# First loads of an S5 + GEGLU kernel: the Gelu table ahead of a weight load on ScalarE, three parameter loads from SyncE to GpSimd

## The chip, the core and the metric

The kernel runs on one core of one Trainium2 chip. A core has TensorE (PE, matmuls), VectorE (DVE), ScalarE (ACT), GpSimd (POOL) and SyncE (SP, which issues DMAs here). ScalarE and GpSimd can issue DMAs too. The metric is device time in microseconds (us); lower is better. The time given for a kernel is the median of its runs.

## The reference, cut to what matters

One batch of L = 2048 rows of D = 512 values is normalized; two branches read the result, and their sum is added to the input.

```python
xn = layernorm(x)                                   # over the 512 values of a row, eps 1e-5
dt = exp(log_dt); Lam_bar = exp(dt * Lam)           # Lam = Lambda_re + 1j * Lambda_im, 512 of them
B_bar = ((Lam_bar - 1) / Lam)[:, None] * Bmat
h[t] = Lam_bar * h[t-1] + B_bar @ xn[t]             # complex recurrence over the 2048 rows
A = 2 * (h @ Cmat.T).real + xn * Dskip
B = (gelu(xn @ w_gate) * (xn @ w_up)) @ w_down      # 512 -> 1376 -> 512
out = x + A + B                                     # bfloat16
```

## The kernel before

**Blocks and stages.** The 2048 rows are four blocks of 512, each of four tiles of 128 rows. For a block b, `LN(b)` computes row statistics (L625, L626), mean and square root (`root`, L628 to L634: a copy and a `pow` on GpSimd, L633 and L632), reciprocal (L637) and the normalized rows XN (`norms`, L644). `TR(b)` transposes these by four DMAs (L722) into XNT[b]. `BU(b)` (L734) multiplies them by B; `CHAIN(b)` turns the recurrence into real scans (L754 to L783, scans at L767) on VectorE. `GU(b)` (L823) makes the gate and up products, and the last 96 of the 1376 columns are made at L797; Gelu and a copy on ScalarE (L838, L841) and a product on VectorE (L843) give the hidden values. `DN(b)` (L863) adds, into PSUM seeded with x, the hidden values times w_down and then the scanned states times C; L881 adds the skip branch and a DMA (L883) stores the tile.

**Block 0 is special.** The start can't wait for DMA transposes. Its tiles are centred (L931, L939; the mean of tile 1 comes from ScalarE, L936), transposed on TensorE (`cent_T`, L673) with the identity tile IDN, and copied by ScalarE (L680). `GT_mm` (L698) then multiplies the centred tiles by the first 896 of 1376 gate and up columns, in "units" of a tile by a column range; `GT_evac` scales by the reciprocal root, applies Gelu (L707) and multiplies (L710). The first gate chunk, columns 0 to 383, comes in two halves of 256 rows of w_gate each (`ld_wg0`, L499). The first four matmuls read half 0, the next four half 1, both for tile 0; eight more multiply tile 1 by gate columns; after these come the up columns (L491). Behind the units TensorE does `GU(0)` for four column tiles, `BU(0)` and `BU(1)`, then `GU(1)` and the rest.

**Set-up.** VectorE sets WRM (L476) and HALF (L478) and makes IDN (L480) from an iota of GpSimd (L479). GpSimd clears the parameter rows PROW (L481) and fills EXB, EPS, HPI, IOTJ and HR (L548 to L552). ScalarE applies Gelu to HALF (L554) early, so that its function table is loaded. TensorE runs seven matmuls on zeros meanwhile (L913).

**Parameters.** `load_par` loads log_dt, Lambda_re and Lambda_im into rows of PROW (L515, 1 KB each); `tr_par` transposes PROW by DMA into PAR (L519). `params` (L567 and on) and `coefs` make the scan's coefficients from it.

**What sets the order.** `Sched` holds all operations with their reads and writes, estimated durations and engine. TensorE's and SyncE's instructions stay in the order in which the code adds them; the others are ordered by a planner, `schedule`, from these durations and from priorities that it works out backward. `emit` writes each engine's program, with a semaphore wait ahead of an operation for each of its producers. A queue is strictly in order: what stands behind a waiting DMA waits with it. `order_behind(op, prev)` keeps an operation behind another of the same engine without a semaphore wait. SyncE's order at the start is: tiles 0 and 1 of x; half 1 of the first gate chunk; tile 2; up chunk 0; tile 3; gate and up chunks 1 and 2; the three parameter loads; gate and up chunks 3; `tr_par`; `TR(0)`; x of block 1 (L485); transposed loads of B_re and B_im (L530); Dskip (L539); x of block 2; `TR(1)`. Half 0 is issued by ScalarE, which waits for IDN first; the Gelu operation has a planner's earliest time of 900 ns (`nb`).

Of the kernel before, what the change touches and what calls it, by code (L numbers as in the profile page):

```python
# [10 lines left out]
ACTF = mybir.ActivationFunctionType  # L11
BF16, F32, I32 = dt.bfloat16, dt.float32, dt.int32
# [347 lines left out]
EPS_BF16 = 1.0013580322265625e-05  # L360
# [6 lines left out]
def d_dve_ts4x(n): return 220.0 + 0.26 * n  # L367
# [5 lines left out]
def build(nc, ins, out):  # L373
    with ExitStack() as es:
        E = es.enter_context
        S = Sched(nc, es)
        ARENA_BYTES = 207 * 1024
        arena_t = E(nc.sbuf_tensor("arena", [128, ARENA_BYTES // 2], BF16))
        A = Arena(arena_t, ARENA_BYTES)
# [6 lines left out]
        WG = A.alloc("WG", [KD, F], BF16)  # L386
# [30 lines left out]
        HALF = A.alloc("HALF", [4], F32)  # L417
# [11 lines left out]
        PROWq = [Buf("PROW%d" % q, "prow", q, q + 1) for q in range(3)]  # L429
# [3 lines left out]
        EXB = A.alloc("EXB", [KP], F32)  # L433
        HPI = A.alloc("HPI", [1], F32)
        EPS = A.alloc("EPS", [1], F32)
# [15 lines left out]
        HR = A.alloc("HR", [4, 128], BF16)  # L451
        HRp = [A.sub(A.alloc("HRv", [2, 256], BF16, at=HR.lo), "HR%d" % i, i) for i in range(2)]
# [8 lines left out]
        IOTJ = A.alloc("IOTJ", [512], I32, at=OUTB_all.lo)  # L461
# [8 lines left out]

        V = lambda fn, dur, r, w, tag="", after=(): S.op("vector", fn, dur, r, w, tag, after)
        ACT = lambda fn, dur, r, w, tag="", after=(): S.op("scalar", fn, dur, r, w, tag, after)
        POOL = lambda fn, dur, r, w, tag="": S.op("gpsimd", fn, dur, r, w, tag)
        PE = lambda fn, dur, r, w, tag="": S.op("tensor", fn, dur, r, w, tag)

        V(lambda e: e.memset(WRM.ap, 0.0), 150, [], [WRM], "wrm")  # L476
        GATE = {"before_gelu": [], "nh": 0}
        V(lambda e: e.memset(HALF.ap, 0.5), D_TINY, [], [HALF], "half")  # L478
        POOL(lambda e: e.iota(IOT.ap, [[1, 128]], base=0, channel_multiplier=-1), 300, [], [IOT], "iota")  # L479
        GATE["ident"] = V(lambda e: e.tensor_scalar(IDN.ap, IOT.ap, 0.0, None, ALU.is_equal), d_dve_ts4x(128), [IOT], [IDN], "ident")  # L480
        POOL(lambda e: e.memset(PROW16.ap, 0.0), 100, [], [PROW, *PROWq], "prow0")  # L481
        NM1 = A.alloc("NM1", [1], F32)
# [11 lines left out]
        def ld_x0(j):  # L494
            S.dma(lambda e, j=j: e.dma_start(X[j].ap, x2[128 * j:128 * (j + 1), :]), 128 * 1024, writes=[X[j]], tag="ld_x0")  # L495
        WG0h = [Buf("WG0h%d" % n, "sbx", n / 2, (n + 1) / 2) for n in range(2)]

        def ld_wg0(n, queue, after=()):
            S.dma(lambda e: e.dma_start(WG.ap[:, 2 * n:2 * n + 2, 0:384],  # L499
                                        ins["B_w_gate"][256 * n:256 * (n + 1), 0:384].rearrange("(k p) f -> p k f", p=128)),  # L500
                  192 * 1024, writes=[WG0h[n]], tag="ld_w", queue=queue, after=after)
        ld_x0(0)
        ld_x0(1)
        ld_wg0(0, "scalar", [GATE["ident"]])
        ld_wg0(1, "sync")
        ld_x0(2)
        ld_w(WU, WUc, ins["B_w_up"], 0)
        ld_x0(3)
# [4 lines left out]
        def load_par():  # L513
            for q, nm in enumerate(("A_log_dt", "A_Lambda_re", "A_Lambda_im")):
                S.dma(lambda e, q=q, nm=nm: e.dma_start(PROW.ap[4 * q:4 * q + 4, :], ins[nm].rearrange("(s p) -> s p", p=128)),  # L515
                      1024, writes=[PROWq[q]], tag="ld_" + nm)

        def tr_par():
            S.dma(lambda e: e.dma_start_transpose(PAR.ap.rearrange("p q t -> p (q t)").unsqueeze(1), PROW16.ap), 4096,  # L519
# [25 lines left out]

        wchunk = lambda ft: 0 if ft < 3 else (1 if ft < 5 else (2 if ft < 7 else 3))

        POOL(lambda e: e.memset(EXB.ap, math.e), 100, [], [EXB], "exb")  # L548
        POOL(lambda e: e.memset(EPS.ap, EPS_BF16), 100, [], [EPS], "eps")
        POOL(lambda e: e.memset(HPI.ap, 0.5 * math.pi), 100, [], [HPI], "hpi")  # L550
        POOL(lambda e: e.iota(IOTJ.ap, [[1, 512]], base=0, channel_multiplier=0), 600, [], [IOTJ], "iotj")
        POOL(lambda e: e.memset(HR.ap, 0.0), 300, [], HRp, "hr0")  # L552
        SCR = A.alloc("SCR", [1], F32)
        GATE["table"] = ACT(lambda e: e.activation(SCR.ap, HALF.ap[:, 0:1], ACTF.Gelu_apprx_tanh), 1480, [HALF], [SCR], "gelu0")  # L554
        GATE["table"].nb = 900.0
        rstate = {"n": 0}

        def next_bank():
# [7 lines left out]
        def params():  # L566
            S.order_behind(POOL(lambda e: e.tensor_tensor(DTB.ap, EXB.ap, LDT.ap, ALU.pow), 1100, [EXB, LDT], [DTB], "exp_dt"), GATE["pow"])  # L567
            V(lambda e: e.tensor_tensor(pa(TH), DTB.ap, LIM.ap, ALU.mult), D_TINY, [DTB, LIM], [PA[TH]], "th")
            V(lambda e: e.tensor_tensor(pa(A_), DTB.ap, LRE.ap, ALU.mult), D_TINY, [DTB, LRE], [PA[A_]], "a")
            POOL(lambda e: e.tensor_tensor(pa(RRr), EXB.ap, pa(A_), ALU.pow), 1100, [EXB, PA[A_]], [PA[RRr]], "exp_a")  # L570
            V(lambda e: e.tensor_scalar(w16(0, 4), pa(TH), 1.0 / TWO_PI, None, ALU.mult), D_TINY, [PA[TH]], [W16p[0]])
            V(lambda e: e.tensor_scalar(w16(4, 8), pa(TH), 512.0 / TWO_PI, None, ALU.mult), D_TINY, [PA[TH]], [W16p[1]])
            V(lambda e: e.tensor_scalar(w16(8, 16), w16(0, 8), 0.25, None, ALU.add), D_TINY, W16p[0:2], W16p[2:4])
            V(lambda e: e.tensor_copy(KI.ap, W16.ap), D_TINY, W16p, [KI])
            V(lambda e: e.tensor_tensor(FRC.ap, W16.ap, KI.ap, ALU.subtract), D_TINY, W16p + [KI], [FRC])
# [34 lines left out]
        def tables_dve(behind):  # L610
            for s in range(KP):
                V(lambda e, s=s: e.tensor_scalar(K1s[s].ap, IOTJ.ap, W16.ap[:, s:s + 1], None, ALU.mult),
                  d_dve_ts4x(512) * 1.3, [IOTJ, W16p[0]], [K1s[s]], "k1", [GATE["evTA"]])
                V(lambda e, s=s: e.scalar_tensor_tensor(F1s[s].ap, IOTJ.ap, W16.ap[:, s:s + 1], K1s[s].ap, ALU.mult, ALU.subtract),  # L614
# [315 lines left out]
        def sub(j):  # L930
            return V(lambda e: e.tensor_scalar(XN[j].ap, X[j].ap, MVt[0][j].ap[:, 0:1], None, ALU.subtract),  # L931
                     d_dve_ts4x(512), [X[j], MVt[0][j]], [XN[j]], "sub")
        load_par()
        load_W()
        tr_par()
# [83 lines left out]
def bass_parallel_sum__ssm_conv_s5__geglu_ffn__prompt_kernel(  # L1019
    nc: bass.Bass,  # L1020
    A_x: bass.AP,
    A_Lambda_re: bass.AP,
    A_Lambda_im: bass.AP,
    A_B_re: bass.AP,
    A_B_im: bass.AP,
    A_C_re: bass.AP,
    A_C_im: bass.AP,
    A_log_dt: bass.AP,
    A_Dskip: bass.AP,
    B_x: bass.AP,  # L1030
    B_w_gate: bass.AP,
    B_w_up: bass.AP,
    B_w_down: bass.AP,
    out: bass.AP,
):
    ins = {
        "A_x": A_x, "A_Lambda_re": A_Lambda_re, "A_Lambda_im": A_Lambda_im,
        "A_B_re": A_B_re, "A_B_im": A_B_im, "A_C_re": A_C_re, "A_C_im": A_C_im,
        "A_log_dt": A_log_dt, "A_Dskip": A_Dskip,
        "B_w_gate": B_w_gate, "B_w_up": B_w_up, "B_w_down": B_w_down,  # L1040
    }
    build(nc, ins, out)
# [28 lines left out]
```

## Time and profile before

| | us |
|---|---|
| median of 5 runs | 180.52 |
| lowest, highest | 179.8, 180.85 |
| profiled execution | 180.85 |
| its span in the trace | 179.0 |
| TensorE busy | 173.2 |
| VectorE busy | 160.7 |
| ScalarE busy | 89.4 |
| GpSimd busy | 14.0 |

The profile is of one execution; the span runs from its first to its last recorded instruction. Times in a row are microseconds from the span's start, unless marked ns. In a row of the order of time, the first number is the start, the second the length, then come engine (a q behind it is its queue, which issues DMAs), line, operation and tiles. In a row of waits the numbers are the sum, the count and the longest. L340 is the place where waits are written for all engines. Matmuls overlap in their pipeline, so TensorE's busy time says less than the chain of work that ended last, which is followed back from the end of the kernel. The granted TensorE clock is full in all slices of the page.

### The profile page before, as it was taken

Reading aid. Unit: us, or ns where it says so; the run is one execution under the profiler, and the core shown is the slowest. Engines: PE = TensorE matmul, PEld = TensorE weight load, DVE = VectorE, ACT = ScalarE, POOL = GpSimd, SP = SyncE. Lnnn points to the kernel's source line nnn. Section 1 sums busy time; section 2 is a strip of 40 time slices with the busy share of each in tenths; the row PEclk is TensorE's granted clock in tenths of the full one; section 3 lists DMA queues with packets and bytes.
Section 4 is the critical chain, followed back from the end, with each engine's and each line's share of the span. In section 5 each row is a group of like instructions: output and inputs, shape, how many; then the busy total and the mean of one; then the engine's idle time right before and its main releaser. Section 6 shows DMA issues by size and latency. Waiting matters only on the chain.

```text
span 179.0 us, 2505 instructions
## 1 busy us (share of the span) xinstructions
PE 173.2 (97%) x884; PEld 83.7 (47%) x884; DVE 160.7 (90%) x283; ACT 89.4 (50%) x169; POOL 14.0 (8%) x25
## 2 busy tenths in 40 slices
PE   7799999699999999999999999999999999999994
PEld 3664364244644444444544444444464444444453
DVE  5798898997999979969999999989999999999911
ACT  3475559987776799101676596000567880000000
POOL 3222040209000000200000000000000000000000
PEclk9999999999999999999999999999999999999999
DMA  5994899697599500001105100010001000000321
GB/s 144 290 311 91 187 196 179 91 118 149 109 225 323 126 4 2 0 29 34 54 13 107 29 2 0 24 39 29 29 0 29 4 0 0 0 0 10 112 78 41
DMA packets 33397, 14.37 MB, mean 80 GB/s; under 512 B 23688, under 2 KB 33384, under 8 KB 33384
## 3 DMA queue, kind: packets, MB, share of 16 engines
q1 hardware_dynamic: 33112, 14.01, 35.0%
q10 hardware_dynamic: 272, 0.20, 0.4%
q8 instruction: 7, 0.11, 0.3%
q14 instruction: 6, 0.05, 0.1%
HBM read 6.46 MB, written 2.10 MB: 48 GB/s over the span
## 4 chain that ended last, share of the span: by engine, by line
PE 84%; DMA 7%; DVE 6%; SPq 1%; issue 1%; ACT 0%; ACTq 0%; DVEq 0%
PE PS L863 37%; PE PS L823 29%; PE PS L734 12%; PE PS L698 4%; DMA arena<-in_B_w_up_dram 3%; DMA arena<-in_A_x_dram 2%; PE PS L797 2%; DMA arena<-arena 2%; DVE arena L625 1%; DVE arena L710 1%; DVE arena L644 1%; DVE arena L614 1%; SPq L495 1%; DVE arena L616 1%; DVE arena L843 0%
## 5 line engine op out<-in xcount | busy, mean ns | idle before, releaser
L863 PE MATMUL PS<-arena 128*128 128x512 bf16 (+3 forms) x323 | 66.2, 366 | 0.0
L823 PE MATMUL PS<-arena 128*128 128x512 bf16 x264 | 58.1, 379 | 0.3 <-DMA arena<-arena 0.3
L863 PEld LDWEIGHTS PS<-arena 128*128 128x128 bf16 (+1 forms) x323 | 30.8, 98 | 35.3
L823 PEld LDWEIGHTS PS<-arena 128*128 128x128 bf16 x264 | 25.7, 98 | 30.9 <-issue 0.7
L767 DVE TENSOR_TENSOR_SCAN arena<-arena 128x512 bf16<-128x512 f32 x32 | 38.7, 1251 | 0.0
L838 ACT ACTIVATE arena<-PS 128x512 bf16<-128x512 f32 x33 | 19.8, 601 | 37.4 <-PE PS L823 33.8
L734 PE MATMUL PS<-arena 128*128 128x512 bf16 x128 | 28.3, 379 | 1.4 <-DMA arena<-arena 1.4
L841 ACT ACTIVATE arena<-PS 128x512 bf16<-128x512 f32 x33 | 19.7, 598 | 5.2 <-PE PS L823 4.9
L734 PEld LDWEIGHTS PS<-arena 128*128 128x128 bf16 x128 | 12.5, 98 | 16.5 <-issue 1.9
L738 ACT ACTIVATE arena<-PS 128x512 bf16<-128x512 f32 x32 | 17.6, 596 | 1.3 <-PE PS L734 1.3
L855 ACT ACTIVATE PS<-arena 128x512 f32<-128x512 bf16 (+2 forms) x17 | 9.3, 580 | 17.8 <-DVE arena L881 17.1
L881 DVE TENSOR_TENSOR arena<-PS,arena 128x512 bf16<-128x512 f32 (+2 forms) x17 | 10.8, 651 | 8.2 <-PE PS L863 8.1
L843 DVE TENSOR_TENSOR arena<-arena 128x512 bf16<-128x512 bf16 x33 | 13.0, 411 | 1.5 <-ACT arena L841 1.5
L698 PE MATMUL PS<-arena 128*128 128x192 bf16 (+2 forms) x80 | 12.8, 315 | 0.4 <-DMA arena<-in_B_w_gate_dram 0.3
L625 DVE BATCH_NORM_STATS2 arena<-arena 128x6 f32<-128x512 bf16 x16 | 10.3, 682 | 2.9 <-DMA arena<-in_A_x_dram 2.9
L698 PEld LDWEIGHTS PS<-arena 128*128 128x128 bf16 x80 | 7.1, 98 | 5.3 <-DMA arena<-in_B_w_gate_dram 0.5
L754 DVE TENSOR_TENSOR arena<-arena 128x4096 bf16<-128x4096 bf16 (+1 forms) x5 | 9.2, 1854 | 0.0
L756 DVE TENSOR_TENSOR arena<-arena 128x4096 bf16<-128x4096 bf16 (+1 forms) x5 | 9.2, 1852 | 0.0
L780 DVE TENSOR_TENSOR arena<-arena 128x4096 bf16<-128x4096 bf16 x4 | 9.1, 2284 | 0.0
L779 DVE TENSOR_TENSOR arena<-arena 128x4096 bf16<-128x4096 bf16 x4 | 9.1, 2283 | 0.0
L707 ACT ACTIVATE arena<-PS,arena 128x192 bf16<-128x192 f32 (+1 forms) x16 | 6.7, 449 | 3.0 <-PE PS L698 2.6
L710 DVE SCALAR_TENSOR_TENSOR arena<-PS,arena 128x192 bf16<-128x192 f32 (+1 forms) x16 | 6.9, 448 | 0.7 <-ACT arena L707 0.4
(84 smaller groups left out, 113.7 us busy)
## 6 DMA issues: line engine op xcount, KB each, us to landing
out_dram<-arena SPq DMA_DIRECT2D x15, 128.0 KB, 1.7
arena<-in_A_x_dram SPq DMA_DIRECT2D x3, 512.0 KB, 5.5
arena<-in_B_w_down_dram SPq DMA_DIRECT2D x1, 1280.0 KB, 7.2
arena<-in_A_x_dram SPq DMA_DIRECT2D x4, 128.0 KB, 2.8
arena<-in_B_w_gate_dram SPq DMA_DIRECT2D x2, 256.0 KB, 5.5
arena<-in_B_w_up_dram SPq DMA_DIRECT2D x2, 256.0 KB, 5.8
arena<-in_B_w_gate_dram SPq DMA_DIRECT2D x1, 480.0 KB, 4.3
arena<-in_B_w_up_dram SPq DMA_DIRECT2D x1, 480.0 KB, 5.2
```

Of the source, the lines that this page charges most:

```text
L625: return (V(lambda e: e.bn_stats(ST[tt].ap, X[tt].ap), d_dve_1x(512), [X[tt]], [ST[tt]], "bnst"), V(lambda e: e.bn_aggr(MVt[b][j].ap, ST[t ...
L698: ins_ = e.matmul(dst, XCd(j, k), WGU[:, us[0]:us[-1] + 1, k, f0:f1], start=(k == 0), stop=(k == KD - 1))
L734: ins_ = e.matmul(PS[bank][:, :], BBT[c][dk].ap[:, 128 * s:128 * (s + 1)], XNT[b].ap[:, dk, :], start=(dk == 0), stop=(dk == KD - 1))
L738: ACT(lambda e, bank=bank, k3=k3, s=s, c=c: e.activation(SSc[k3][s][c].ap, PS[bank][:, :], ACTF.Copy), d_act(512), [BANK[bank]], [SSc[k3][ ...
L767: V(lambda e, g=g, rb=rb, init=init: e.tensor_tensor_scan(g.ap, rb, g.ap, init, ALU.mult, ALU.add), d_dve_scan(512), [g, PA[RRr]] + ([CARc ...
L823: ins_ = e.matmul(PS[bank][0:m, c0:c1], W.ap[:, dk, 128 * ft:128 * ft + m], XNT[b].ap[:, dk, c0:c1], start=(dk == 0), stop=(dk == KD - 1))
L838: GATE["last_gelu"] = ACT(lambda e, bg=bg, kk=kk, m=m: e.activation(GG[kk].ap[0:m, :], PS[bg][0:m, :], ACTF.Gelu_apprx_tanh), d_act(512), ...
L841: ACT(lambda e, bu=bu, kk=kk, m=m: e.activation(UPB[kk].ap[0:m, :], PS[bu][0:m, :], ACTF.Copy), d_act(512), [BANK[bu]], [UPB[kk]], "evU")
L843: V(lambda e, kk=kk, m=m, ft=ft, k2=k2: e.tensor_tensor(HTt[k2][ft].ap[0:m, :], GG[kk].ap[0:m, :], UPB[kk].ap[0:m, :], ALU.mult), d_dve_tt ...
L855: ACT(lambda e: e.activation(PS[bank][:, c0:c1], X[tt].ap[:, c0:c1], ACTF.Copy), d_act(c1 - c0), [X[tt]], [BANK[bank]], "seed")
L863: ins_ = e.matmul(PS[bank][:, c0:c1], l_[:, 128 * j:128 * (j + 1)], r_[:, c0:c1], start=False, stop=last and n == len(ops) - 1, skip_group ...
L881: V(lambda e: e.tensor_tensor(OUTB[ko].ap[:, c0:c1], PS[bank][:, c0:c1], XD[tt].ap[:, c0:c1], ALU.add), d_dve_1x(c1 - c0), [BANK[bank], XD ...
```

## The change

The Gelu operation that loads ScalarE's table moves to the start of the program and becomes ready with HALF; its earliest time of 900 ns goes. Half 0 of the first gate chunk is issued by SyncE, in half 1's old place; half 1 is issued by ScalarE, in order behind the Gelu operation, without waiting for IDN. The three parameter loads are issued by GpSimd. GpSimd's EXB, EPS, HPI, IOTJ and HR wait for IDN. What is computed is the same.

```diff
-        POOL = lambda fn, dur, r, w, tag="": S.op("gpsimd", fn, dur, r, w, tag)
+        POOL = lambda fn, dur, r, w, tag="", after=(): S.op("gpsimd", fn, dur, r, w, tag, after)
...
+        SCR = A.alloc("SCR", [1], F32)
         V(lambda e: e.memset(HALF.ap, 0.5), D_TINY, [], [HALF], "half")
+        GATE["table"] = ACT(lambda e: e.activation(SCR.ap, HALF.ap[:, 0:1], ACTF.Gelu_apprx_tanh), 1480, [HALF], [SCR], "gelu0")
...
         def ld_wg0(n, queue, after=()):
-            S.dma(lambda e: e.dma_start(WG.ap[:, 2 * n:2 * n + 2, 0:384],
+            return S.dma(lambda e: e.dma_start(WG.ap[:, 2 * n:2 * n + 2, 0:384],
...
-        ld_wg0(0, "scalar", [GATE["ident"]])
-        ld_wg0(1, "sync")
+        ld_wg0(0, "sync")
+        S.order_behind(ld_wg0(1, "scalar"), GATE["table"])
...
-                      1024, writes=[PROWq[q]], tag="ld_" + nm)
+                      1024, writes=[PROWq[q]], tag="ld_" + nm, queue="gpsimd")
...
-        POOL(lambda e: e.memset(EXB.ap, math.e), 100, [], [EXB], "exb")
-        POOL(lambda e: e.memset(EPS.ap, EPS_BF16), 100, [], [EPS], "eps")
-        POOL(lambda e: e.memset(HPI.ap, 0.5 * math.pi), 100, [], [HPI], "hpi")
-        POOL(lambda e: e.iota(IOTJ.ap, [[1, 512]], base=0, channel_multiplier=0), 600, [], [IOTJ], "iotj")
-        POOL(lambda e: e.memset(HR.ap, 0.0), 300, [], HRp, "hr0")
-        SCR = A.alloc("SCR", [1], F32)
-        GATE["table"] = ACT(lambda e: e.activation(SCR.ap, HALF.ap[:, 0:1], ACTF.Gelu_apprx_tanh), 1480, [HALF], [SCR], "gelu0")
-        GATE["table"].nb = 900.0
+        POOL(lambda e: e.memset(EXB.ap, math.e), 100, [], [EXB], "exb", [GATE["ident"]])
+        POOL(lambda e: e.memset(EPS.ap, EPS_BF16), 100, [], [EPS], "eps", [GATE["ident"]])
+        POOL(lambda e: e.memset(HPI.ap, 0.5 * math.pi), 100, [], [HPI], "hpi", [GATE["ident"]])
+        POOL(lambda e: e.iota(IOTJ.ap, [[1, 512]], base=0, channel_multiplier=0), 600, [], [IOTJ], "iotj", [GATE["ident"]])
+        POOL(lambda e: e.memset(HR.ap, 0.0), 300, [], HRp, "hr0", [GATE["ident"]])
```

## The prediction

> **What bounds the kernel now.** I read the page first, then the chain that ended last, then TensorE's waits, then the order of time of the first 40 us on the queues of SyncE, ScalarE, GpSimd and VectorE.
>
> ```profile
> span 179.0 us, 2505 instructions
> PE 173.2 (97%) x884; PEld 83.7 (47%) x884; DVE 160.7 (90%) x283; ACT 89.4 (50%) x169; POOL 14.0 (8%) x25
> ...
> PE 84%; DMA 7%; DVE 6%; SPq 1%; issue 1%; ACT 0%; ACTq 0%; DVEq 0%
> ```
>
> A busy share of 97% is not yet a bound, since ends of matmuls are modelled. The chain says it better: from 34.39 to 176.77 us it lies on TensorE without a gap, 142.4 us. So the time is the moment at which BU(1) begins (34.39), plus a fixed 142.4, plus the last store. What the change touches lies wholly ahead of that moment. TensorE's waits:
>
> ```profile
> PE PS L734 <- DMA arena<-arena: 1.4, 1, 1.4
> ...
> PE PS L698 <- DMA arena<-in_B_w_gate_dram: 0.3, 1, 0.3
> PE PS L823 <- DMA arena<-arena: 0.3, 1, 0.3
> ```
>
> The chain gives a fourth: 2.63 us issue of the first up chunk (WU chunk 0), landing 5.04 later, at 7.67; TensorE goes on at 7.72. After 7.72 only 0.27 us (GU(0) for the transposes of TR(0)) and 1.39 us (BU(1) for those of TR(1)) are idle. These two are all that can be won behind 7.72, 1.66 us. What holds the transposes is SyncE's queue:
>
> ```profile
> 7.12 0.79 SPq L515 DMA_DIRECT2D arena<-in_A_log_dt_dram  x1
> ...
> 7.96 0.26 SPq L515 DMA_DIRECT2D arena<-in_A_Lambda_re_dram  x1
> ...
> 8.26 0.29 SPq L515 DMA_DIRECT2D arena<-in_A_Lambda_im_dram  x1
> 8.59 0.40 SPq L491 DMA_DIRECT2D arena<-in_B_w_gate_dram  x1
> ...
> 9.03 0.51 SPq L491 DMA_DIRECT2D arena<-in_B_w_up_dram  x1
> ...
> 11.68 1.17 SPq L519 DMA_TRANSPOSE arena<-arena  x1
> ```
>
> ```profile
> 12.89 5.18 SPq L722 DMA_TRANSPOSE arena<-arena  x4
> 18.12 0.58 SPq L485 DMA_DIRECT2D arena<-in_A_x_dram  x1
> 18.75 3.48 SPq L530 DMA_TRANSPOSE arena<-in_A_B_re_dram  x1
> 22.27 3.18 SPq L530 DMA_TRANSPOSE arena<-in_A_B_im_dram  x1
> 25.49 0.58 SPq L539 DMA_DIRECT2D arena<-in_A_Dskip_dram  x1
> 26.11 0.43 SPq L485 DMA_DIRECT2D arena<-in_A_x_dram  x1
> 26.59 5.25 SPq L722 DMA_TRANSPOSE arena<-arena  x4
> ```
>
> ```profile
> SPq L340 <- DMA arena<-in_A_Lambda_im_dram: 2.0, 1, 2.0
> ```
>
> The reader is to see an in-order queue: three parameter loads at 7.12 to 8.55, a stand of 2.0 us until the last of them has landed, the parameters' transpose, and everything later back to back behind it. Each of the four transposes of TR(1) starts when the one before ends (26.59, 27.84, 29.14, 30.58), and the last lands at 34.14, so the queue and not the normalized rows is late.
>
> **The parameter loads leave SyncE.** Three issues go (7.12 to 8.59, 1.47 us), and with them the stand of 2.0 us, if the parameters land in time. The last two weight chunks then issue from 7.12; the 1.82 us issue at 5.25 and the 0.79 at 7.12 show a queue held up until about 7.9, so they end between 8.06 and, an estimate with one more 0.9 us stall, 9.0. The parameters' transpose (1.17) ends by 9.3 to 10.2. Next late are the normalized rows: L644 ends at 10.23, 11.27, 11.91, 13.07. TR(0), at 1.30 apart as now, issues from 10.3 instead of 12.89 and ends at 15.5 instead of 18.07: 2.6 earlier. TR(0) then lands about 17, under the units that keep TensorE busy to 19.16: the 0.27 goes.
>
> The next load of x issues at 15.5 and lands, with today's 4.29, at 19.8. VectorE's statistics of it, now at 22.44 after 0.70 us idle, can begin at 21.74, where the work ahead ends: 0.70 earlier, not 2.6. The rows ready at 25.91, 26.97, 28.16 and 29.23 come at 25.2, 26.3, 27.5 and 28.5. SyncE gets there at 24.0, so TR(1) now waits for rows: 25.2, 26.5, 27.8, 29.1. The last lands after 2.5 us (the median of L722) to 3.56 (today's): 31.6 to 32.7. BU(0) ends at 33.0 - 0.27 = 32.73. The 1.39 goes, with 0.1 to 1.1 us to spare.
>
> **Gate halves.** SyncE issues one half at 1.66 before and after; it is now the one that the first matmuls read (landing 3.5 later, about 5.2, instead of 6.12). The other issues on ScalarE behind the table. The tile the table reads is ready at about 0.98; load 1.28 and activation 0.20 (rows L554) give 2.5 for the issue at the latest, 1.0 if the queue runs ahead; landing after 3.8, by 6.3. Behind it lie 12 narrow matmuls, some 1.0 us, so TensorE is ready at 7.3, before WU chunk 0 at 7.67. SyncE's place for that chunk (2.63) does not move. Cost and gain nothing; without that cover, 1 us for each us past 6.7.
>
> **Table first.** The row-1 mean on ScalarE, at 4.19 right behind the table's activation, can start when its rows land, about 0.4 earlier. VectorE's 0.75 us wait for it shrinks. Hidden behind the same 7.67; nothing.
>
> **GpSimd.** Today it is idle from 2.36 to 6.24. Three issues enter behind the memset at 1.20, and the set-up (0.09, 0.54, 0.51, 0.17, 0.14: 1.45) follows them. Behind it waits the first `pow` (with the copy, 0.94; ends 7.18), then reciprocal, row statistics 3, the first gate evacuation and the transposes of tile 3 (10.57). Slack along it: 0.32 + 0.41 + 0.66 = 1.4. No row shows a DMA issued by GpSimd. [...]
>
> [...]
>
> **Sum.** 180.85 (profiled execution: span 179.0 and 1.85 around it) - 0.27 - 1.39 = 179.19. That execution is 0.33 above the median, so 178.9. VectorE must follow: its last states end at 163.54, and TensorE reads them at 143.87 + 16.42 (DN(2), 76 matmuls, 0.216 each) + 22 x 0.216 = 165.0, 1.5 us of slack; it gains 0.70 and the 1.13 idle at 31.67, so it does.
>
> **Rivals.**
> [...]
> 2. A wait takes the other's place. The parameters land late, or TR(1) still misses 32.73, or statistics stay at 22.44: only 0.3 to 0.8 is won, 180.0. For it: the last landing has 0.1 us to spare with 3.56.
> 3. The order that the planner writes changes. Costs and ready times that it is given alter, and VectorE is 90% busy with 1.5 us of slack: its work late by over 1.5 + 1.66 would cost; 1 us more gives about 181.7. Against: in its own costs the weights' transfer sets TR(0), so VectorE's order has little reason to move.
> 4. Hidden anyway: nothing moves, 180.5. Against: BU(1) does wait 1.39.
>
> **How the numbers follow.** Forecast 0.57; rival 2 0.14, rival 4 0.06; rival 1 0.12, rival 3 0.11. About 0.5% (0.9 us) is what a measurement of this kernel can tell from no change. Below 179.6: the forecast, 0.57 (its own range 178.3 to 179.5). Within: rivals 2 and 4, 0.20. Above 181.4: rivals 1 and 3, 0.23. The range reaches through rival 2 and most of rival 3: 178.2 to 182.0, leaving out rival 1 and the end of rival 3, about 0.15, above, and 0.04 below.
>
> **What would show it.** No L515 on SyncE and no wait for Lambda_im; first L722 near 10.3, load of x near 15.5, TR(1) from about 25.2; BU(1) near 32.7, without DMA wait; TensorE's first up matmul still near 7.7; `pow` not later than 7.2. Wrong if L632 on GpSimd ends past 8.6, if L722 starts past 12, or if L863 waits for VectorE.

## The result, and the profile after

| | before | after |
|---|---|---|
| median, us (runs) | 180.57 (80) | 179.17 (43) |
| lowest to highest | 179.25 to 183.04 | 178.83 to 180.99 |
| profiled execution | 180.85 | 180.96 |
| its span | 179.0 | 179.1 |

The ratio of after to before over the runs is 0.9946, interval 0.9933 to 0.9959: faster by 0.54%. Seven of the 80 executions before, at 182.51 and above, are of a slower state (its granted clock was 0.991 where it was recorded) and are not in the ratio. The forecast was 178.9. The table holds a puzzle: the median falls by 1.40 us, while the profiled execution is no shorter than that of before. The 43 times lie in two groups with nothing between them: 31 from 178.83 to 179.60 (median 179.01) and 12 from 180.47 to 180.99 (median 180.6). The profiled execution is one of the upper group. So its trace shows what was removed, and also something that the prediction did not have.

The page of after:

```profile
span 179.1 us, 2505 instructions
...
PE 174.9 (98%) x884; PEld 86.0 (48%) x884; DVE 160.0 (89%) x283; ACT 89.3 (50%) x169; POOL 12.4 (7%) x28
...
PEclk9999999999999999999999999999999999999999
...
PE 95%; DMA 2%; ACT 0%; DVE 0%; SPq 0%; issue 0%; DVEq 0%
```

TensorE's share of the chain rises from 84 to 95%, that of DMA falls from 7 to 2%. After, TensorE's list of waits holds these and nothing else of 0.2 us or more:

```profile
PE PS L912 <- DVE arena L479: 1.0, 1, 1.0
...
PE PS L672 <- DVE arena L938: 0.4, 1, 0.4
...
PE PS L672 <- DVE arena L930: 0.2, 1, 0.2
```

The first of them is the warm-up's, for its zeros, and stands in the kernel before too. No wait for a DMA is left: those of `BU(1)` (1.4) and of `GU(0)` (0.3) are gone. SyncE's queue in the order of time, after (L521 is `tr_par`, L721 `TR`, L487 the load of x):

```profile
7.69 0.69 SPq L493 DMA_DIRECT2D arena<-in_B_w_up_dram  x1
8.51 1.31 SPq L521 DMA_TRANSPOSE arena<-arena  x1
11.62 6.26 SPq L721 DMA_TRANSPOSE arena<-arena  x4
17.92 0.58 SPq L487 DMA_DIRECT2D arena<-in_A_x_dram  x1
...
26.82 5.12 SPq L721 DMA_TRANSPOSE arena<-arena  x4
```

`tr_par` starts at 8.51 instead of 11.68, with no stand for Lambda_im. `TR(0)` nevertheless starts only at 11.62, and `TR(1)` at 26.82, later than before (26.59). It is not the queue that is late now but the rows that it moves: VectorE, which makes them, stands for TensorE's first units. VectorE after (L709 evacuates a unit, L643 makes normalized rows):

```profile
10.85 0.42 DVE L709 SCALAR_TENSOR_TENSOR arena<-PS,arena 128x192 bf16<-128x192 f32 x1 [1.76 <-PE PS L697]
11.18 0.41 DVE L643 TENSOR_SCALAR arena<-arena 128x512 bf16<-128x512 bf16 x1
```

So TensorE is late. TensorE in the order of time, after:

```profile
5.57 0.61 PE L672 MATMUL PS<-arena 128*128 128x128 bf16 x4 [0.42 <-DVE arena L938]
5.97 3.41 PE L697 MATMUL PS<-arena 128*128 128x192 bf16 x20
9.17 0.63 PE L672 MATMUL PS<-arena 128*128 128x128 bf16 x4
9.59 2.81 PE L697 MATMUL PS<-arena 128*128 128x192 bf16 x20
...
20.67 5.34 PE L822 MATMUL PS<-arena 128*128 128x512 bf16 x24
...
27.17 13.11 PE L733 MATMUL PS<-arena 128*128 128x512 bf16 x60
```

The same of before:

```profile
5.41 0.40 PE L673 MATMUL PS<-arena 128*128 128x128 bf16 x4 [0.50 <-DVE arena L939]
6.12 2.10 PE L698 MATMUL PS<-arena 128*128 128x192 bf16 x20 [0.31 <-DMA arena<-in_B_w_gate_dram]
8.06 0.39 PE L673 MATMUL PS<-arena 128*128 128x128 bf16 x4
...
19.43 5.34 PE L823 MATMUL PS<-arena 128*128 128x512 bf16 x24 [0.27 <-DMA arena<-arena]
...
25.93 7.07 PE L734 MATMUL PS<-arena 128*128 128x512 bf16 x32
34.39 5.99 PE L734 MATMUL PS<-arena 128*128 128x512 bf16 x27 [1.39 <-DMA arena<-arena]
```

The first twenty narrow matmuls take 3.41 us in one and 2.10 in the other (0.26 of it a wait for the up chunk), and the single matmuls of 192 columns are spaced 0.160 us against 0.082: TensorE runs at about half rate until about 10 us in this execution of after, and until about 5 in this one of before (first group of transposes 0.61 for four, second 0.40). The page's row of the granted clock shows full speed in both throughout, but it counts a stretch without a record as full. The trace's own record of this clock begins, at full, at 10.32 us in after and at 5.32 in before, which is where the spacing changes. `BU` begins 1.24 late (27.17 against 25.93), then runs through without the wait at 34.39. The gain of 1.55 and this loss of 1.24 nearly cancel in the profiled execution, and 0.4 more at the end (below) does the rest.

### The profile page after: what moved, and what is told of

Its sections match the earlier page's. It is cut to its first block, busy times and chain, and to the rows that moved or that the text cites. A ratio compares the mean times of both kernels' runs of the same rounds, so it can differ in the third digit from the quotient of the medians.

```text
span 179.1 us, 2505 instructions
## 1 busy us (share of the span) xinstructions
PE 174.9 (98%) x884; PEld 86.0 (48%) x884; DVE 160.0 (89%) x283; ACT 89.3 (50%) x169; POOL 12.4 (7%) x28
## 4 chain that ended last, share of the span: by engine, by line
PE 95%; DMA 2%; ACT 0%; DVE 0%; SPq 0%; issue 0%; DVEq 0%
PE PS L862 37%; PE PS L822 32%; PE PS L733 15%; PE PS L697 8%; PE PS L796 3%; DMA arena<-in_A_x_dram 2%; PE PS L672 1%; ACT arena L935 0%; SPq L497 0%; DVE arena L938 0%; DVE arena L880 0%; DVEq L340 0%
## 5 line engine op out<-in xcount | busy, mean ns | idle before, releaser
L822 PEld LDWEIGHTS PS<-arena 128*128 128x128 bf16 x264 | 25.7, 98 | 30.5
L733 PEld LDWEIGHTS PS<-arena 128*128 128x128 bf16 x128 | 12.5, 98 | 14.8
L697 PE MATMUL PS<-arena 128*128 128x192 bf16 (+2 forms) x80 | 14.6, 352 | 0.0
L624 DVE BATCH_NORM_STATS2 arena<-arena 128x6 f32<-128x512 bf16 x16 | 10.2, 678 | 1.4 <-DMA arena<-in_A_x_dram 1.4
L697 PEld LDWEIGHTS PS<-arena 128*128 128x128 bf16 x80 | 9.0, 115 | 4.6
L709 DVE SCALAR_TENSOR_TENSOR arena<-PS,arena 128x192 bf16<-128x192 f32 (+1 forms) x16 | 6.9, 448 | 2.7 <-PE PS L697 1.8
```

Source lines behind the costliest of these rows:

```text
L624: return (V(lambda e: e.bn_stats(ST[tt].ap, X[tt].ap), d_dve_1x(512), [X[tt]], [ST[tt]], "bnst"), V(lambda e: e.bn_aggr(MVt[b][j].ap, ST[t ...
L697: ins_ = e.matmul(dst, XCd(j, k), WGU[:, us[0]:us[-1] + 1, k, f0:f1], start=(k == 0), stop=(k == KD - 1))
L733: ins_ = e.matmul(PS[bank][:, :], BBT[c][dk].ap[:, 128 * s:128 * (s + 1)], XNT[b].ap[:, dk, :], start=(dk == 0), stop=(dk == KD - 1))
L822: ins_ = e.matmul(PS[bank][0:m, c0:c1], W.ap[:, dk, 128 * ft:128 * ft + m], XNT[b].ap[:, dk, c0:c1], start=(dk == 0), stop=(dk == KD - 1))
```

## The experiments

What was to be told apart: (a) the parameters' leaving SyncE carries the whole gain, and the two-group pattern is a moment of TensorE's clock that any execution can draw; (b) some part of the change makes that moment late; (c) the gain is not what the sum says, since the table or the gate halves take part.

### The change again, and its parts one at a time

The changed kernel once more, no edit.

> The changed kernel again, for a second trace. In the trace of after, the first twenty 128x192 matmuls of L697 took 3.2 us (0.160 each, half rate), where those of before took 2.1 with a 0.33 us wait. Rate theory: TensorE begins at half rate and goes over to full rate at a moment that differs between executions; where it comes early, times lie near 178.9 to 179.4 (span about 177.2), where it comes late near 180.5 to 181.0; a trace of the earlier kind shows those twenty in 1.6 to 2.1 us and GU(0) starting near 19.2. Queue theory (rival): transfers or GpSimd's set-up are late in the slower executions; then a trace of the faster kind has the same matmul rate, and an earlier landing instead.

Measured: 179.02 (178.91 to 181.11, 22 runs), ratio 0.9949 [0.9925, 0.9973]. Again two groups, 15 up to 179.14 and 7 from 180.28. With the first 43, the upper group holds 19 of 65 executions. The profiled one (180.81) was again of the upper group and again had the twenty matmuls in 3.41.

Only the parameter part: the loads on GpSimd, its other set-up behind the identity; table and gate halves as before. It was measured twice, with 11 and 6 executions. The edit, against the kernel before:

```diff
-                      1024, writes=[PROWq[q]], tag="ld_" + nm)
+                      1024, writes=[PROWq[q]], tag="ld_" + nm, queue="gpsimd")
...
-        POOL(lambda e: e.memset(EXB.ap, math.e), 100, [], [EXB], "exb")
+        POOL(lambda e: e.memset(EXB.ap, math.e), 100, [], [EXB], "exb", [GATE["ident"]])
```

(and the other four likewise).

> The kernel before with the parameter part alone: the three loads issued by GpSimd, its set-up behind IDN; table and gate halves as before. Queue account: SyncE's 2.0 us stand goes, TR(0) begins near 10 in an execution with an early full rate, both waits of TensorE (0.27 and 1.39) go, so the faster executions lie at 178.9 to 179.3, and a part still lies near 180.5 to 181. If the gain came from the gate halves and the table instead: 180.5, as before. The end, from the landing of the last store to the end of the span, was 0.43 us in before and 0.79 in all kernels with the loads on GpSimd; if these loads are its cause it is 0.8 here.

> The parameter part alone once more. Its first trace had TensorE idle for 0.26 us between the transposes of tile 0 and tile 1, where the two traces of after had 0.42 and 0.65, because row 1's mean on ScalarE began at 3.99 instead of 4.32. If that gap decides how often the full rate comes late, few or none of the executions lie above 180.3 again (0 of 11 the first time); if it was chance, about 3 in 10.

Measured: 179.16 (178.57 to 179.51), ratio 0.994 [0.9917, 0.9963], and 179.05 (178.85 to 179.47), ratio 0.9924 [0.9897, 0.995]. No upper group in 17 executions, where the first expectation had one. TensorE in the second one's profile (span 177.0):

```profile
4.54 1.03 PE L673 MATMUL PS<-arena 128*128 128x128 bf16 x8 [0.17 <-DVE arena L931]
5.50 2.28 PE L698 MATMUL PS<-arena 128*128 128x192 bf16 x20
7.62 0.39 PE L673 MATMUL PS<-arena 128*128 128x128 bf16 x4
...
25.06 13.98 PE L734 MATMUL PS<-arena 128*128 128x512 bf16 x62
38.87 1.46 PE L823 MATMUL PS<-arena 128*128 128x512 bf16 x6
```

and its queue of SyncE:

```profile
8.40 1.32 SPq L519 DMA_TRANSPOSE arena<-arena  x1
9.81 5.14 SPq L722 DMA_TRANSPOSE arena<-arena  x4
15.01 0.58 SPq L485 DMA_DIRECT2D arena<-in_A_x_dram  x1
...
24.71 5.13 SPq L722 DMA_TRANSPOSE arena<-arena  x4
```

This is the execution that the prediction described: `TR(0)` at 9.81, x at 15.01, `TR(1)` at 24.71, and from 4.54 on TensorE without a wait. In the first profile the up chunk came later (a wait of 0.80) and these three stand at 10.56, 15.80 and 25.38. The parameter part alone carries the whole gain. It has two pieces, which were not tried apart: the loads leave SyncE, and with the set-up out of the way the identity ends at 1.33 instead of 2.30, so that half 0 goes out at 1.36 instead of 2.33. The queue's rows tie the gain to the first piece.

Only the other part: table first and gate halves swapped; the parameters stay on SyncE, and GpSimd's set-up doesn't wait. The edit, against the changed kernel (the five set-up operations, not shown, lose their wait too):

```diff
-                      1024, writes=[PROWq[q]], tag="ld_" + nm, queue="gpsimd")
+                      1024, writes=[PROWq[q]], tag="ld_" + nm)
```

> The kernel before with the ScalarE part alone: Gelu table first, gate halves exchanged; parameter loads on SyncE and GpSimd's set-up as before. Queue account: the stand of 2.0 us for Lambda_im and BU(1)'s wait for the transposes of TR(1) remain, since SyncE is not earlier: 180.2 to 180.7, and what TensorE gains ahead of GU(0) (0.3 to 0.7) turns into a longer wait. If the ScalarE part carries the gain: 179.0 to 179.5. The end of the span behind the last landing is 0.43.

Measured: 180.28 (179.55 to 180.72, 22 runs), ratio 0.9998 [0.9982, 1.0014]: nothing. The wait of `BU(1)` is there as before:

```profile
34.09 6.20 PE L733 MATMUL PS<-arena 128*128 128x512 bf16 x28 [1.51 <-DMA arena<-arena]
```

So (c) falls: table and halves bring no time of their own.

### The half-rate start

If the moment of full rate is what splits the times, then taking away TensorE's warm-up on zeros should make nearly every execution late, in the changed kernel and in the kernel before.

```diff
-        nwarm = 7
+        nwarm = 1
```

> The changed kernel with 1 instead of 7 matmuls on zeros at the start. Rate theory: TensorE is now at half rate in all executions until some 8 to 11 us, so the faster group is gone: 180.2 to 181.5, and GU(0) starts at 20.3 to 21.5. Queue theory: matmuls on zeros move no data and no queue, so the times stay as they are, mostly 179.0.

> The kernel before with 1 instead of 7 matmuls on zeros. Rate theory: the late full rate costs about 1.4 us up to GU(0), but BU(1) waits for the transposes of TR(1) until 34.1 anyway, so most is absorbed: 180.4 to 181.2, at most 0.6 above before. Queue theory: no difference from before, 180.5.

Measured on the changed kernel: 180.36 (179.67 to 181.16, 22 runs), ratio 0.9991 [0.9975, 1.0007]: the gain is gone, though the three loads are off SyncE. Seven executions lie below what was expected, five of them at 179.67 to 179.83, between the two groups. On the kernel before: 180.64 (180.08 to 181.41, 14 runs), ratio 1.0007 [0.999, 1.0024]: no loss. TensorE in this last profile (kernel before, short warm-up):

```profile
5.82 3.41 PE L698 MATMUL PS<-arena 128*128 128x192 bf16 x20
...
27.35 12.90 PE L734 MATMUL PS<-arena 128*128 128x512 bf16 x59
```

The same 3.41 for the twenty, `BU` 1.42 later than in the kernel before, and no wait at `BU(1)`. That is the asymmetry. Before, a late TensorE runs into rows that land at 34.14 anyway, and its lateness is swallowed by the wait. After, there is no wait left to swallow it.

The opposite edit: six more matmuls of 128 columns on zeros around the first transposes, so that TensorE has hardly a gap between 4 and 6 us. On the changed kernel twice (6 and 10 runs), on the kernel before once.

```diff
-        fill(2)
+        fill(4)
         cent_T(0, tb, "AA")
+        fill(4)
         cent_T(1, [wb])
```

> The changed kernel with 6 more small matmuls on zeros at the start: four instead of two ahead of the transposes of tile 0, and four between those of tile 0 and tile 1, where TensorE stood idle for 0.17 and 0.42 us. Rate theory: a fuller start brings the full rate sooner, so fewer or none of the executions lie above 180.3, and the median falls to 178.9 to 179.1. Queue theory: no difference from after.

> The changed kernel with the denser start once more, since 6 executions are too few for a share. Rate theory: at most 1 in 10 above 180.3, median 178.9 to 179.1. If the six were chance: about 3 in 10 above 180.3, as in after.

> The kernel before with the same 6 more small matmuls on zeros. Rate theory: the early full rate is there in more executions, but BU(1) still waits for TR(1): 180.2 to 180.6, no gain over before beyond 0.3. Rival: the denser start is itself the gain of a4, whatever the queues do: then 179.0 to 179.5 here too.

Measured on the changed kernel: 179.0 (178.91 to 179.27), ratio 0.9911 [0.989, 0.9933], and 179.04 (178.83 to 180.06), ratio 0.9923 [0.99, 0.9946]. None of 16 above 180.2. On the kernel before: 180.25 (178.97 to 181.54, 14 runs), ratio 0.9993 [0.9969, 1.0016], the filling alone is worth nothing there; its profiled execution had another wait, 2.48 us of `GU(0)` for the transposes of `TR(0)`. TensorE in the second profile of the filled changed kernel (span 177.0):

```profile
5.54 2.24 PE L697 MATMUL PS<-arena 128*128 128x192 bf16 x20
...
25.05 3.19 PE L733 MATMUL PS<-arena 128*128 128x512 bf16 x13
```

It agrees with the parameter part alone to 0.01 us at `BU`. With the upper group's share of 19 in 65, the chance that 16 executions hold none is 0.71 to the 16th, 0.004; for the 17 of the parameter part, 0.003. The profiled executions say the same one by one. Where the trace's record of the clock turns to full at 4.56, 4.65, 6.29 and 6.51, in kernels with the parameters off SyncE, the times are 178.91, 179.51, 179.37 and 178.85; where it turns at 8.97, 9.47, 9.81, 10.32 and 10.32, they are 180.27, 180.50, 180.81, 180.96 and 180.93. So the upper group is the late full rate, and (a) is right only by half: something in the whole change makes it more frequent than the parameter part does.

### Which part makes it frequent

GpSimd's set-up now lies at 3.23 to 4.52 and could disturb the first centring on VectorE. GpSimd's rows after:

```profile
1.51 0.70 POOL L517 DMA_DIRECT2D arena<-in_A_log_dt_dram  x1 [0.30 <-POOL arena L483]
2.21 0.52 POOL L517 DMA_DIRECT2D arena<-in_A_Lambda_re_dram  x1
2.72 0.52 POOL L517 DMA_DIRECT2D arena<-in_A_Lambda_im_dram  x1
3.23 0.13 POOL L550 MEMSET arena<- 128x4 f32 x1
3.29 0.58 POOL L553 IOTA arena<- 128x512 int32 x1
3.79 0.55 POOL L554 MEMSET arena<- 128x512 bf16 x1
```

and VectorE's after:

```profile
1.10 0.23 DVE L482 TENSOR_SCALAR arena<-arena 128x128 bf16<-128x128 int32 x1 [0.16 <-POOL arena L481]
...
3.72 0.77 DVE L930 TENSOR_SCALAR arena<-arena 128x512 bf16<-128x512 bf16 x1
```

The identity (L482) falls from 1.20 to 0.23, since the iota and the fills no longer lie beside it; the centring of tile 0 (L930) rises from 0.35 to 0.77, where they now lie. To see whether this matters, the set-up was put behind the centring of tile 1.

```diff
-        POOL(lambda e: e.memset(EXB.ap, math.e), 100, [], [EXB], "exb", [GATE["ident"]])
+        POOL(lambda e: e.memset(EXB.ap, math.e), 100, [], [EXB], "exb", [sub1])
```

(and the other four likewise, added behind that operation, `sub1`).

> The changed kernel with GpSimd's set-up (EXB, EPS, HPI, IOTJ, HR) waiting for the centred rows of tile 1 (L938) instead of IDN. In after L930 took 0.77 us beside that set-up, where before it took 0.35, and TensorE stood 0.17 us more ahead of tile 0. [...] If those 0.2 us decide how often the full rate comes late, fewer than 3 in 10 of the executions lie above 180.3; if they do not matter, the share stays near 3 in 10 and the median at 179.0 to 179.2.

Measured: 179.36 (179.15 to 180.98, 22 runs), ratio 0.9966 [0.9943, 0.9989]. The centring is back at 0.35 in its profile, yet 8 of 22 executions lie above 180.2. The set-up's new place is not the cause. The lower group is some 0.3 higher (179.15 to 179.39); the one profile is of the upper group, so no row explains it.

Next, the parameters off GpSimd altogether: issued by ScalarE right behind half 1 of the first gate chunk (moved there after planning, so that the order of all else stays).

```diff
         S.schedule()
+        for op in [o for o in S.order["gpsimd"] if o.kind == "dma"]:
+            S.order["gpsimd"].remove(op)
+            op.eng = "scalar"
+            q = S.order["scalar"]
+            q.insert(max(n for n, o in enumerate(q) if o.kind == "dma" and o.start < 4000.0) + 1, op)
```

> The changed kernel with the three parameter loads moved on, from GpSimd to ScalarE's queue, directly behind half 1 of the gate chunk; the planner's order is otherwise that of after. Queue account: what counts is that they left SyncE; both waits of TensorE stay gone, faster executions at 179.0 or below. For the end of the span (0.79 us behind the last landing in all kernels with loads issued by GpSimd, 0.40 to 0.43 in the others): if GpSimd's loads are the cause it is 0.4 here and the faster executions lie at 178.5 to 178.7; if the shorter program of SyncE is, it stays 0.8 and they lie at 178.9 to 179.1. Slower executions near 180.2 to 180.6 remain in about 3 of 10.

The same with the filling of TensorE as above:

> The same with the 6 more small matmuls on zeros at the start. If both accounts hold (early full rate in nearly all executions, 0.4 us less at the end), this is the fastest kernel of the study: 178.5 to 178.7, with at most 1 in 10 of the executions above 180. If the end does not depend on GpSimd's loads: 178.9 to 179.1.

Measured: 180.22 (179.0 to 180.84, 22 runs), ratio 0.9967 [0.9944, 0.9989], 11 of 22 above 180.2, where about 3 in 10 were expected; and, filled, 179.37 (178.96 to 180.04, 11 runs), ratio 0.9944 [0.9922, 0.9967], none above 180.2. That was expected at 178.5 to 178.7, or at 178.9 to 179.1 if the end of the program doesn't depend on GpSimd's loads; both were missed. In its profile the rows of tile 1 came later than in any other trace, at 4.72. ScalarE is not a better place than GpSimd.

| kernel | above 180.2 | idle ahead of tile 1's transposes, us (profiled) | gate half issued on ScalarE at | clock's record turns to full at |
|---|---|---|---|---|
| after, two profiles | 19 of 65 | 0.42, 0.65 | 1.00 (half 1) | 10.32, 9.81 |
| set-up behind `sub1` | 8 of 22 | 0.70 | 0.99 | 10.32 |
| parameters on ScalarE | 11 of 22 | 0.75 | 1.00 | 8.97 |
| parameter part alone, two profiles | 0 of 17 | 0.26, 0 | 1.36 (half 0) | 4.65, 6.51 |
| after, filled, two profiles | 0 of 16 | 0.28, 0 | 0.99 | 4.56, no record |
| parameters on ScalarE, filled | 0 of 11 | 0.53 | 0.99 | 6.29 |
| table and halves alone | hidden by the wait | 0.90 | 0.99 | no record; spacing full from 3.88 |

The late executions go with ScalarE's part of the change (38 of 109 with it and unfilled, 0 of 17 without), and more work for TensorE ahead of about 6 us removes them (0 of 27 in the two filled kernels). The idle time alone doesn't decide: the last two rows have 0.53 and 0.90 of it and are early.

What decides is where the idle time falls. In the eleven traces with a record of the clock, its stretch at full lasts 170.67 us or 174.08, which is 50 or 51 times 3.413. So in these traces the clock changes on a grid of 3.413 us, and the grid lies elsewhere from one execution to another: counted from the span's start, the turns fall at 0.06 to 3.10 us of a step. With idle counted from the spacing (an estimate), TensorE stood for 0.76 us or less in the 3.413 ahead of the turn, in all eleven; in every earlier step of the grid, at whose end the clock did not turn, it had stood for 0.90 or more. In after the step from 3.50 to 6.91 holds 1.00 (0.38 ahead of the transposes of tile 0, 0.62 ahead of those of tile 1), and the clock turns one step later, at 10.32. In the filled kernel before, the grid lies within 0.02 us of the same place, the step holds 0.58, and the clock turns at 6.89. Where the grid lets a step end before the second gap, as at 4.65 in the parameter part alone, the gap does no harm. On this reading, which rests on the traces and on no experiment that set the grid, only some executions are late because the grid falls differently; and moving the set-up changed little because the idle time only moved: the gap ahead of tile 0 shrank to 0.11 and the one ahead of tile 1 grew to 0.91, since tile 1 came no sooner.

With ScalarE's part, tile 1's mean on ScalarE waits for the load of tile 1. It begins at 4.06 to 4.72 in all nine traces in which ScalarE issues a gate half by 1.00 (4.32 in after, 2.09 idle for x), and at 3.99 and 3.38 in the two of the parameter part alone, where the half goes out at 1.36. SyncE issues tile 1 at 1.19. That the load is late because the half goes out ahead of it is argued from these times and was not tried by itself; the filled after began at 4.20 and 4.06, so the landing itself varies too.

## Why the prediction was right, and where its sum was off

**The bound** was read rightly: take the waits at `GU(0)` and `BU(1)` away and all behind them moves up. With the parameters off SyncE both are gone in every profile; with them on SyncE and full warm-up, that of `BU(1)` is there (1.39; 1.51 with table and halves alone) or another for the transposes.

**The size, "GU(0) 0.27 and BU(1) 1.39", was too small.** An idle time in the trace begins at the modelled end of the last matmul, but the next could start before that: rows of 512 columns are 0.379 long and 0.216 apart. Before, `BU(0)` begins at 25.93, so its 32 matmuls allow `BU(1)` at 25.93 + 32 x 0.216 = 32.84; it came at 34.39, 1.55 late. For `GU(0)`, the forty of L698 ahead of it take 8.64 from 10.79 before, and 8.21 from 12.46 after: 0.43. The waits were worth 1.98, not 1.66.

**The sum left out the end of the program.** VectorE's last rows, before:

```profile
176.80 0.29 DVE L881 TENSOR_TENSOR arena<-PS,arena 128x128 bf16<-128x128 f32 x1 [0.41 <-PE PS L863]
```

and in the parameter part alone (second profile):

```profile
174.38 0.29 DVE L881 TENSOR_TENSOR arena<-PS,arena 128x128 bf16<-128x128 f32 x1 [0.41 <-PE PS L863]
```

From the end of this row to the end of the span lie 1.9 us before (177.09 to 179.0) and 2.3 in the other (174.67 to 177.0). "Plus the last store" was taken as fixed; it grew by 0.4. SyncE's wait for the stores before:

```profile
SPq L345 <- DMA out_dram<-arena: 0.2, 1, 0.2
```

after:

```profile
SPq L345 <- DMA out_dram<-arena: 0.7, 2, 0.5
```

All ten profiles with the parameters off SyncE have the second form, those with the loads on ScalarE too, where GpSimd issues no DMA; all four with them on SyncE have the first. So it goes with the loads' leaving SyncE, whose program is three issues shorter, and not with GpSimd's queue. What costs the time is open.

With both corrections the sum closes. In the second profile of the parameter part, GU(1) begins at 38.87 against 41.29, 2.42 earlier: 1.98 for the waits and 0.44 because the first up chunk landed earlier (the tile-2 transposes, behind it, at 7.62 against 8.06). Less 0.4 at the end: 2.0, as the spans show (179.0, 177.0). The chunk's landing isn't part of the change: in the first profile of the same kernel TensorE waited 0.80 for it and those transposes came at 8.29. For the medians: 180.57 - 1.98 + 0.39 = 178.98, against 179.01 for the lower group. That they agree to 0.03 is partly chance: the waits are those of one execution, and the executions before spread over 2 us. The predicted 178.9 was close by luck as well: an under-counted wait (0.32) and an uncounted end (0.4) nearly cancelled.

**What the prediction did not have: the half-rate start.** It adds about 1.6 to 12 of 43 executions (median 180.6 against 179.01), and is why the ratio is 0.9946 and the medians alone would give 0.9922. The traces show TensorE at half rate first (matmuls of 192 columns spaced 0.160 us against 0.082), its clock turning on the grid of 3.413, and the moment of the turn differing between executions (clock full from between 4.56 and 10.32). 1.6 of 180 is 0.9%, as much as the whole change. It was visible in the profile before, in the 0.61 of the first transposes, and was passed over because waits behind it hid it there.

**Point by point.**
- *SyncE's queue.* Predicted `tr_par` ended by 9.3 to 10.2, `TR(0)` from 10.3, x at 15.5, `TR(1)` from 25.2 with SyncE waiting for rows. In the early execution of the parameter part they were 9.72, 9.81, 15.01 and 24.71. TensorE's 0.44 earlier transposes account for most of the difference, and SyncE, free at 23.87, did wait for rows.
- *Gate halves, "cost and gain nothing".* Right in the common execution (table and halves alone: ratio 0.9998; lower group of after 179.01, parameter part alone 179.05 and 179.16). Wrong in the cover: 7.67 for the up chunk was taken as the moment that hides all; what lies ahead of it also sets the clock's moment, and there the part has a price. In after the first up matmul came at 8.53, not near 7.7.
- *Table first.* The mean of tile 1 was to start 0.4 earlier than 4.19. It started at 4.32: its rows, and no longer the table, come last.
- *GpSimd.* Before, no row showed a DMA issued by it, so the 0.12 for rival 1, GpSimd late, rested on the author's estimate; no run shows GpSimd late by its issues. They took 0.70, 0.52 and 0.52, landing in 3.2 to 3.7, the last (issued at 2.72) before SyncE's `tr_par` at 8.51. GpSimd's set-up ended at 4.52. The copy ahead of the `pow` (L632 in after) then waited 1.87 us for VectorE, so rival 1 had no part; the `pow` ended at 7.34 in after, past the 7.2 named as a sign, because tile 1 was late. Beside the three issues (1.51 to 3.24) VectorE ran statistics alone, from 2.77; what an issue costs beside other work of VectorE is not shown.
- *GpSimd's set-up beside VectorE.* It held VectorE up by 0.42 at the centring of tile 0 (0.77 against 0.35). Moving it shows that it does not decide the time.
- *Rival 3, the planner's order.* In the traces VectorE, ScalarE and TensorE run the same operations in the same order before and after. Excluded. *Rival 2* (180.0, a wait in the other's place) did not come as described, but in its kind: lateness of TensorE in the place of the wait for the queue, in 3 executions of 10.

No version tried is clearly faster than the common execution of after. Filling TensorE, or leaving ScalarE's part out, removes the slower executions.

## What to carry to other kernels

A small load in SyncE's in-order queue cost its issue plus the stand behind it: three loads of 1 KB, 1.47 us of issues and a stand of 2.0, held transposes back by some 3 us (`TR(0)` at 12.89 against 9.81), and GpSimd's queue took them (0.70, 0.52 and 0.52 an issue) at no price on the path. When the last wait that a chain ran into is removed, everything ahead of it begins to count, the rate of TensorE's start included (here 1.6 us in 12 of 43 executions). So look at the spacing of its first matmuls before such a change, close the gaps between them, and look for groups in the times after it. Measure a wait from where the next matmul could have started, not from the row's end.

## What had not been expected of the hardware

- The moment of full rate splits one kernel's executions into 179.0 and 180.6. In the eleven traces with a record of it, it falls on a grid of 3.413 us; there 0.76 us of idle time in a step (counted from the spacing, an estimate) still let the clock turn, 0.90 did not. The page's row of the granted clock doesn't show it. Six matmuls of 128 columns on zeros removed the second group (0 of 16 against 19 of 65).
- ScalarE's queue issued a DMA at 1.00 that stands behind the Gelu operation in the program, while that operation's table load ran from 0.73 to 2.01: the issue did not wait for the work ahead of it. The prediction had left open whether it would (1.0 or 2.5).
- The end of the program was 0.4 us longer in every profile in which SyncE issued three DMAs fewer.
- An iota and a fill on GpSimd lengthened VectorE's `tensor_scalar` beside them: 0.23 to 1.20 for 128x128, 0.35 to 0.77 for 128x512.
